# Attention and max-out FFN on one core: weighted sums two beats earlier in the first pairs, small bound products moved, GpSimd tied to the row maxima, first batch's maxima in SBUF

## The chip, the core and the metric

The kernel runs on one NeuronCore of a Trainium2 chip. The metric is the device time in microseconds (us). Before the change three runs took 1024.45, 1021.29 and 1019.76 us, with a median of 1021.29 us.

## The reference

Inputs are `q`, `k`, `v` of shape (8, 12, 448, 64), gains `g_q`, `g_k` of 64, and four 768 x 768 matrices. All are float32.

```python
q_n, k_n = rmsnorm(q, g_q), rmsnorm(k, g_k)       # over the last axis, eps 1e-6
scores = q_n @ k_n.T / 8
attn = exp(scores - rowmax); attn /= sum + 1e-9
x = (attn @ v), heads put side by side            # (8 * 448, 768)
h = max(x @ w1, x @ w2, x @ w3)
out = h @ w_out
```

## The kernel before

**Pairs and beats.** Two heads of one batch make a *pair*; there are 48, six to a batch. The program is one Python loop that writes the instructions of all five engines by hand, in order: each pair `g` has 12 *beats* `i`, and `beat(g, i)` (L1085) issues what is due there. `later(n, work)` puts a small step n beats on; those steps come at the end of their beat, in `tick`, and the ones marked `True` come last there. Each engine then takes its own instructions strictly in that order, so the order on each engine is the schedule, and the tile framework adds the semaphores between them.

**One pair.** The 448 query rows of a pair go in four chunks `c`, three beats each: three of 128 rows by two heads, and a last one in which 64 rows of each head share a tile (`banks(c)` is 1). For a chunk, `scores` (L655) lets TensorE write the score tile `sc` to PSUM (two buffers in all), `row_max` (L688) lets VectorE find the negated row maxima `nm`, and `softmax` (L697) lets ScalarE take the exponentials and row sums.

**The first six pairs** (`g < PLAIN`) run in float32, without the split in two terms. Their exponentials `e` are turned by TensorE (`turn_plain` L719, tiles `turned`), copied to `pt` by ScalarE (`keep_turned` L735), and multiplied with the values (`add_values` L832, tile `av`); q and k rows are turned likewise (`turn_whole` L522, tiles `rows`). The row sums are spread by small products (`spread_sums` L758), VectorE scales `av` (`scale_plain` L856), and `finish` (L861) writes the two float16 terms of the result, `xt`, on ScalarE and VectorE. All the small PSUM tiles (`turned`, `rows`, `spread`, `marks`, `most` and the FFN's `acc`) share one pool of three buffers, tag `m`, taken in turn. **The other 42 pairs** use float16 in two terms, and DMA does the turning; there a `sc` buffer is free only after VectorE's `lower_weights` (L802, instruction L806).

**Norms.** GpSimd squares the rows of pair g+2 (`squares`, L443), VectorE sums them (`sum_squares`, L450), GpSimd takes the inverse root (`inv_rms`: a scale at L460 and a power at L464) and scales the rows (`scale_rows`, L472).

**Weights.** While the first pairs run, 24 blocks of weights are decoded. A block comes in one DMA (`load_raw`), ScalarE rebiases it (L182), VectorE decodes it in three steps (L190, L194, L199). Every third block `bound_in` (L260) computes a bound: 18 small products into `marks` (L274), a row maximum (L162), a one-column product `most` (L283), a clear (L288) and a power on GpSimd (L293). Then ScalarE and VectorE split the three blocks in two float16 terms (L303, L306). `bound_block` and `bound_out` do the like for `w_out`, and `largest_v` with `bound_v` (L560, L589) for each batch of values: 12 products per half batch (L586), and a one-column product `most` (L597).

**FFN.** `thirds` (L993) feeds FFN steps to TensorE between the attention's steps; the first batch's FFN is queued at pair 6, beat 6, so until then TensorE has nothing but attention and bounds to do. `layer1` (L875) makes 18 units; for each, `hidden` (L887) takes the maximum of three products: the first is copied to SBUF (`m`, L890), the second is joined in `m`, the third is joined in the PSUM tile `acc` itself (L894), which L900 and L904 then read for the two terms of `ht`. So the third `acc` keeps its PSUM buffer until L904 has read it. `layer2` (L933) multiplies with `w_out` (L942).

## Time and profile before

| | |
|---|---|
| median of three runs | 1021.29 us (1019.76 to 1024.45) |
| the profiled execution: its own time, its span | 1023.19 us, 1021.3 us |
| TensorE busy (matmul) | 983.2 us, 96% |
| VectorE, ScalarE, GpSimd busy | 693.2, 624.1, 600.9 us |
| mean granted TensorE clock | 0.984 |
| TensorE busy in 0 to 240 us | 208.2 us |
| TensorE busy in 240 to 1021.3 us | 775.0 of 781.3 us |

The profile is one execution of the program. A row of the timeline has a start, a duration, the engine, the line of the program, `out<-in` and the shapes, and in brackets how long the engine had been idle before it and what released it. In the grouped view a row gives busy time and the mean of one instruction in ns, then the idle time just before the group. A windows row gives for a stretch of time the busy time of each engine, the granted TensorE clock (1.00 is full) and the DMA share. PE is TensorE, PEld its weight loads, DVE VectorE, ACT ScalarE, POOL GpSimd.

### The profile page before, as it was taken

How to read it: one execution, taken by the hardware profiler on the slowest of the kernel's cores; microseconds unless marked ns; L12 is line 12 of the kernel's file. 1: busy time of each engine (PE TensorE's matmuls, PEld its weight loads, DVE VectorE, ACT ScalarE, POOL GpSimd, SP SyncE). 2: the span in 40 equal slices, each digit the busy share in tenths (PEclk: the TensorE clock that was granted, in tenths of full speed). 3: DMA queues.
4: the chain of work that ended last, by engine and by line, in shares of the span. 5: the costliest groups of instructions: out<-in, count | busy, mean ns of one | idle time of the engine just before them, and what ended most of it. 6: DMA issues, size and time to landing. Idle time of an engine off the chain costs nothing. (4 is left out here: it accounts for less than half of the span.)

```text
span 1021.3 us, 17511 instructions
## 1 busy us (share of the span) xinstructions
PE 983.2 (96%) x6045; PEld 528.8 (52%) x6045; DVE 693.2 (68%) x1341; ACT 624.1 (61%) x1419; POOL 600.9 (59%) x659
## 2 busy tenths in 40 slices
PE   8987789899999999999999999999999999999998
PEld 5554444445555555555555555555555555555554
DVE  6998998788667767776677666776767757660120
ACT  6787776477566676666656675667666666651111
POOL 7666786567666576666676765776666657310000
PEclk9998799899999999999999999999999999999999
DMA  9955899979989899999989999999989998851001
GB/s 241 232 165 156 192 177 206 162 136 173 203 170 176 164 210 191 171 175 179 195 162 180 171 195 185 184 165 184 197 154 181 177 195 137 144 94 56 1 1 62
DMA packets 519548, 165.94 MB, mean 162 GB/s; under 512 B 494436, under 2 KB 515236, under 8 KB 519460
## 3 DMA queue, kind: packets, MB, share of 16 engines
q1 hardware_dynamic: 456480, 148.83, 75.3%
q10 hardware_dynamic: 62980, 16.00, 8.4%
q8 instruction: 48, 0.79, 0.3%
q14 instruction: 40, 0.33, 0.1%
HBM read 53.28 MB, written 11.01 MB: 63 GB/s over the span
## 5 line engine op out<-in xcount | busy, mean ns | idle before, releaser
L880 PE MATMUL acc<-xt,w_sb 128*128 128x448 f16 x2592 | 516.0, 354 | 3.6 <-DVE ht L904 3.3
L880 PEld LDWEIGHTS <-w_sb 128*128 128x128 f16 x2592 | 251.4, 98 | 246.4 <-issue 18.0
L709 ACT ACTIVATE sc<-sc,nm 128x448 f32<-128x448 f32 x294 | 178.8, 608 | 190.0 <-DVE nm L693 185.4
L693 DVE TENSOR_REDUCE nm<-sc 128x2 f32<-128x896 f32 x192 | 186.2, 970 | 102.2 <-PE sc L671 59.5
L796 ACT ACTIVATE pp<-sc,rs 128x448 f16<-128x448 f32 x294 | 173.0, 633 | 79.1 <-ACT sc L709 36.3
L806 DVE SCALAR_TENSOR_TENSOR pp<-sc,rs,pp 128x448 f16<-128x448 f32 x294 | 188.0, 675 | 1.7 <-ACT pp L796 1.6
L464 POOL TENSOR_TENSOR ri<-ri,half_neg 128x7 f32<-128x7 f32 x96 | 146.5, 1526 | 8.0
L942 PE MATMUL acc<-w_sb,ht 128*128 128x384 f16 x864 | 147.9, 326 | 0.0
L498 POOL TENSOR_TENSOR kp<-kn,kp 128x448 f16<-128x448 f32 x42 | 43.6, 1037 | 161.4 <-ACT kp L492 154.8
L671 PE MATMUL sc<-kt,qt 128*128 128x448 f16 x504 | 116.7, 354 | 4.0 <-DVE pp L806 3.2
L942 PEld LDWEIGHTS <-ht 128*128 128x128 f16 x864 | 83.7, 98 | 59.2 <-issue 3.9
L671 PEld LDWEIGHTS <-qt 128*128 128x128 f16 x504 | 49.0, 98 | 50.2 <-issue 4.9
L851 PE MATMUL av<-pt,vp 128*64 128x448 f16 x672 | 73.0, 355 | 1.7 <-DMA pt<-pp 1.7
L909 POOL COPY hx<-ht 128x128 f16<-128x128 f16 x48 | 15.4, 321 | 95.0 <-DVE ht L904 93.9
L866 DVE SCALAR_TENSOR_TENSOR xt<-av,xt 128x448 f16<-128x448 f32 x42 | 26.2, 625 | 59.8 <-ACT xt L865 59.8
L638 POOL TENSOR_TENSOR vp<-vr,vp 128x512 f16<-128x512 f32 x42 | 50.0, 1192 | 21.0 <-ACT vp L632 21.0
L450 DVE TENSOR_REDUCE ss<-sq 128x7 f32<-128x448 f32 x96 | 57.7, 601 | 6.4 <-ACT sq L441 4.3
L498 POOL TENSOR_TENSOR qp<-qn,qp 128x448 f16<-128x448 f32 x42 | 45.6, 1086 | 22.8 <-ACT qp L492 21.8
L851 PEld LDWEIGHTS <-vp 128*64 128x64 f16 x672 | 36.0, 109 | 35.8 <-issue 16.7
L460 POOL TENSOR_SCALAR ri<-ss 128x7 f32<-128x7 f32 x54 | 17.8, 329 | 60.4 <-DVE ss L450 59.7
L894 DVE TENSOR_TENSOR m<-acc,m 128x448 f32<-128x448 f32 x48 | 29.5, 615 | 33.2 <-PE acc L880 33.0
L900 ACT ACTIVATE ht<-acc 128x448 f16<-128x448 f32 x48 | 26.2, 546 | 41.8 <-DVE acc L894 41.8
(136 smaller groups left out, 1189.3 us busy)
## 6 DMA issues: line engine op xcount, KB each, us to landing
raw<-in_moe_w_dram SPq DMA_DIRECT2D x18, 768.0 KB, 5.2
kt<-kt SPq DMA_DIRECT2D x84, 112.0 KB, 2.5
out_dram<-osb SPq DMA_DIRECT2D x24, 384.0 KB, 2.7
vr<-in_v_dram SPq DMA_DIRECT2D x42, 192.0 KB, 4.2
kr<-in_k_dram ACTq DMA_DIRECT2D x34, 224.0 KB, 3.6
qr<-in_q_dram ACTq DMA_DIRECT2D x34, 224.0 KB, 4.4
raw<-in_moe_w_out_dram SPq DMA_DIRECT2D x6, 768.0 KB, 5.1
vs<-vp SPq DMA_DIRECT2D x84, 48.0 KB, 2.3
```

Source lines behind the costliest of these rows:

```text
L450: nc.vector.tensor_reduce(sums[g % 2][:, KQ[what]], sq, axis=AX, op=ALU.add)
L464: nc.gpsimd.tensor_tensor(out=ri, in0=ri, in1=half_neg[:, at], op=ALU.pow)
L498: nc.gpsimd.tensor_tensor(out=parts[:, :, 1], in0=n, in1=parts[:, :, 0], op=ALU.subtract)
L638: nc.gpsimd.tensor_tensor(out=vp[:, 1], in0=values_of(g).rearrange("p h n d -> p (h n) d"), in1=vp[:, 0], op=ALU.subtract,)
L671: nc.tensor.matmul(sc[:, h, :S], qt[:, 4 * h + c], kt[:, n, keys[h]], start=n == 0, stop=n == 1,)
L693: nc.vector.tensor_reduce(nm[:, :n], sc[:, :n, :S], axis=AX, op=ALU.max, negate=True)
L709: nc.scalar.activation(to, sc[:, h, :S], AF.Exp, bias=nm[:, h:h + 1], accum_out=total,)
L796: nc.scalar.activation(pp[:, h, 0], sc[:, h, :S], AF.Copy, scale=rs[:, h:h + 1])
L806: nc.vector.scalar_tensor_tensor(out=pp[:, h, 1], in0=sc[:, h, :S], scalar=rs[:, h:h + 1], in1=pp[:, h, 0], op0=ALU.mult, op1=ALU.subtract,)
L851: nc.tensor.matmul(av[half, :S], values, pt[:, 7 * h + block, SHIFT[h]:SHIFT[h] + S], start=n == 0, stop=n == len(steps) - 1,)
L880: nc.tensor.matmul(acc[:, :S], wt[:, wp, c], xs[c][:, xp], start=(c == 0 and n == 0), stop=(c == NCT - 1 and n == 2),)
L942: nc.tensor.matmul(acc[:, :HW], lhs, wo_sb[:, f, wp, half * HW:(half + 1) * HW], start=(f == 0 and n == 0), stop=(f == NFT - 1 and n == 2),)
```

## The change

It has four parts.

1. **Weighted sums two beats sooner.** In the first pairs `add_values` comes at beat 2 of the next pair and not at beat 4. For that the last chunk is turned at beat 11 of its own pair (it was beat 0 of the next), and `keep_turned` of it comes at beat 0, ahead of the next pair's first exponentials on ScalarE.
2. **Small products moved.** `bound_in`'s one-column product and its clear come two beats later, and with them the splits L303 and L306; `bound_block` and `bound_out` come one to three beats later; `largest_v` of the first batch comes two or three beats later. `bound_v` of the later batches starts six beats sooner (beat 7 of the pair ahead), and its product comes four beats after its maximum instead of two.
3. **GpSimd follows the row maxima.** In the first six pairs, ahead of each `row_max`, VectorE clears one element (`here`) and GpSimd copies it, so that what stands behind that copy on GpSimd starts when VectorE starts the row maximum. The squares, inverse roots and scaled rows are re-dealt to the beats with a row maximum, one large GpSimd step behind each copy.
4. **First batch's maxima in SBUF.** For batch 0 the third join writes to `m` in SBUF instead of `acc`, and L900 and L904 (L909 and L913 after) read `m`.

```diff
+    def follow():
+        here = sb.tile([1, 1], F32, name="here", bufs=4)
+        nc.vector.memset(here, 0.0)
+        nc.gpsimd.tensor_copy(seen, here)
...
-            later(8, bound_out, True)
+            later(10, bound_out, True)
...
-        later(6, products)
-        later(8, lambda: row_largest(o_row[:, ft:ft + 1], box[0][:, 0:P]), True)
+        later(7, products)
+        later(9, lambda: row_largest(o_row[:, ft:ft + 1], box[0][:, 0:P]))
...
-        for at, work in ((2, products), (4, reduce), (5, spread), (7, clear)):
+        for at, work in ((2, products), (4, reduce), (7, spread), (9, clear)):
...
-        for at, work in ((2, across), (3, spread), (5, scale)):
+        for at, work in ((2, across), (4, spread), (6, scale)):
...
-        later(2, spread)
-        if b < SQUARED:
-            later(3, clear)
-        later(5 if b < SQUARED else 3, scale)
+        if b >= SQUARED:
+            later(4, spread)
+            later(5, scale)
+            return
+        for at, work in zip((4, 6, 9) if b else (2, 3, 5), (spread, clear, scale)):
+            later(at, work)
...
-        most = m if j == 1 else acc[:, :S]
+        most = m if j == 1 or b == 0 else acc[:, :S]
...
+        if i == 0 and 0 < g <= PLAIN:
+            keep_turned(w, 3)
...
-            if 0 < k <= 4 * PLAIN:
-                turn_plain(*divmod(k - 1, 4))
+            if g < PLAIN:
+                if c > 0:
+                    turn_plain(g, c - 1)
...
+                if g < PLAIN:
+                    follow()
                 row_max(*divmod(k + 1, 4))
...
-        if w >= 0 and i == (4 if w < PLAIN else 7):
+        if w >= 0 and i == (2 if w < PLAIN else 7):
             add_values(w)
...
+        if g < PLAIN:
+            if i in (2, 5):
+                squares(n, "kq"[i // 3])
+            if i == 11:
+                turn_plain(g, 3)
+            if i in (4, 7):
+                sum_squares(n, "kq"[i // 7])
+            if i in (5, 8):
+                if i == 8:
+                    scale_rows(n, "k")
+                inv_rms(n, "kq"[i // 8])
+            if i == (9 if n >= PLAIN else 11):
+                scale_rows(n, "q")
+        elif n < G:
...
-            later(8, lambda: largest_v(i // 3))
+            later(10 if i == 0 else 11, lambda: largest_v(i // 3))
...
-        if g == 1 and i == 1:
+        if g == 1 and i == 4:
             bound_v(0)
-        if g > 1 and g % NP == 0 and g < G and i == 1:
-            bound_v(g // NP)
+        if g % NP == NP - 1 and g + 1 < G and i == 7:
+            bound_v(g // NP + 1)
```

**What moves on the engines.** TensorE, where pair 3 ends and pair 4 begins (`sc` are scores, `turned` the turned exponentials, `rows` the turned k, `most` the bound's product, `av` the weighted sum). Before:

```order
L663 MATMUL sc<-kt,qt 128x448 x2
L729 MATMUL turned<-ident,e 112x128 x8
L663 MATMUL sc<-kt,qt 128x448 x2
L729 MATMUL turned<-ident,e 112x128 x4
L527 MATMUL rows<-ident,kn 128x128 x3
L532 MATMUL rows<-ident,kn 64x64 x2
L663 MATMUL sc<-kt,qt 128x448 x2
L729 MATMUL turned<-ident,e 112x128 x8
L840 MATMUL av<-pt,vr 64x448 x8
```

After, at the same place:

```order
L672 MATMUL sc<-kt,qt 128x448 x2
L738 MATMUL turned<-ident,e 112x128 x8
L290 MATMUL most<-most,ones_c 128x1
L738 MATMUL turned<-ident,e 112x128 x4
L672 MATMUL sc<-kt,qt 128x448 x2
L534 MATMUL rows<-ident,kn 128x128 x3
L539 MATMUL rows<-ident,kn 64x64 x2
L849 MATMUL av<-pt,vr 64x448 x8
L672 MATMUL sc<-kt,qt 128x448 x2
```

The weighted sum now stands ahead of the third score tile, which needs the new pair's first exponentials; the last four turns stand ahead of the second score tile; and `most`, which stood ahead of the first of these rows, has moved between the turns.

GpSimd, one pair's worth in the middle of the first six pairs. Before:

```order
L460 TENSOR_SCALAR ri<-ss_129 128x7
L464 TENSOR_TENSOR ri<-ri,half_neg 128x7
L472 TENSOR_TENSOR kn<-kr,ri 128x448
L472 TENSOR_TENSOR qn<-qr,ri 128x448
L293 TENSOR_TENSOR w_up<-most,half_neg 128x1
L294 TENSOR_SCALAR w_up<-w_up 128x1
L443 TENSOR_TENSOR sq<-kr 128x448
L443 TENSOR_TENSOR sq<-qr 128x448
```

After:

```order
L450 TENSOR_TENSOR sq<-kr 128x448
L165 COPY seen<-here 1x1
L450 TENSOR_TENSOR sq<-qr 128x448
L467 TENSOR_SCALAR ri<-ss_130 128x7
L471 TENSOR_TENSOR ri<-ri,half_neg 128x7
L165 COPY seen<-here 1x1
L479 TENSOR_TENSOR kn<-kr,ri 128x448
L467 TENSOR_SCALAR ri<-ss_130 128x7
L471 TENSOR_TENSOR ri<-ri,half_neg 128x7
L165 COPY seen<-here 1x1
L479 TENSOR_TENSOR qn<-qr,ri 128x448
```

The large steps stood in twos; now each has a copy of its own ahead of it, and that copy waits for VectorE.

More of the change, by code (lines that the diff above doesn't have):

```diff
@@ L158, in qknorm_attention_maxout_ffn_kernel @@
     sums = [const.tile([P, 2 * UNITS], F32, name=f"ss{i}") for i in range(2)]
+    seen = const.tile([1, 1], F32, name="seen")
+    def follow():
+        here = sb.tile([1, 1], F32, name="here", bufs=4)
+        nc.vector.memset(here, 0.0)
+        nc.gpsimd.tensor_copy(seen, here)
     def row_largest(dst, src):
@@ L1096, in beat @@
                 scores(*divmod(k + 1, 4))
-            if 0 < k <= 4 * PLAIN:
-                turn_plain(*divmod(k - 1, 4))
+            if g < PLAIN:
+                if c > 0:
+                    turn_plain(g, c - 1)
+            elif k == 4 * PLAIN:
+                pass
             elif 0 < k <= 4 * G:
@@ L1101, in beat @@
         if part == 1:
-            if 0 < k <= 4 * PLAIN:
-                keep_turned(*divmod(k - 1, 4))
+            if c > 0 and g < PLAIN:
+                keep_turned(g, c - 1)
             if PLAIN <= g < G:
@@ L1125, in beat @@
         thirds(of[i] + (len(queue) > 1 and i % 6 == 4))
-        if w >= 0 and i == (9 if w < PLAIN else 10):
+        if w >= 0 and i == (9 if 0 < w < PLAIN else 10):
             finish(w, x_of[w // NP])
@@ L1148, in beat @@
             upper_rows(n, "k")
-        if n < G:
+        if g < PLAIN:
[12 more added lines that the diff above has]
+        elif n < G:
             if i in (0, 3):
```

## The prediction

> **What bounds the kernel now.** I read the busy time of four stretches, then TensorE's waits up to 320 us, then the timeline at the longest of them, then the groups of VectorE's instructions.
>
> ```profile
> 25.20:118.60 93.40, 81.10 (x580) 46.30 (x580) 86.41 (x120) 73.45 (x164) 63.40 (x56) 0.91 0.70 181
> 118.60:134.00 15.40, 10.28 (x64) 6.60 (x64) 14.62 (x28) 10.38 (x25) 9.76 (x9) 0.78 0.84 201
> 134.00:240.00 106.00, 96.21 (x581) 49.22 (x581) 91.00 (x172) 70.49 (x151) 73.72 (x76) 0.97 0.93 173
> 240.00:1021.30 781.30, 774.98 (x4676) 412.89 (x4672) 485.52 (x990) 454.12 (x1047) 434.70 (x496) 1.00 0.84 156
> PE sc L663 <- ACT e L709: 11.4, 6, 2.9
> PE most L597 <- DVE v_most L591: 4.9, 1, 4.9
> PE marks L586 <- DMA vr<-in_v_dram: 1.6, 2, 1.2
> PE marks L586 <- DVE o_up L342: 1.3, 1, 1.3
> PE most L337 <- DVE o_most L333: 0.8, 1, 0.8
> ```
>
> The four windows rows give span, then busy PE, PEld, DVE, ACT, POOL, then clock. From 240 us on TensorE stands still for only 781.3 - 775.0 = 6.3 us, so nothing the change does there can bring much. Pairs 1 to 5 lie in 25.2 to 118.6: there VectorE is the fullest (86.4 of 93.4 us), TensorE has 81.1, and the clock is at 0.91. The whole kernel ends when TensorE has done its fixed work, so every us that TensorE loses early, standing or at a low clock, is lost at the end.
>
> The timeline shows what one such wait is:
>
> ```profile
> 46.56 3.23 PE L840 MATMUL av<-pt,vr 112*64 112x448 f32 x16
> 76.02 1.02 PE L663 MATMUL sc<-kt,qt 64*128 64x448 f32 x4
> 81.22 1.87 PE L663 MATMUL sc<-kt,qt 64*128 64x448 f32 x4 [2.54 <-ACT e L709]
> 98.33 1.08 ACT L742 COPY pt<-turned 112x512 f32<-112x512 f32 x2
> 99.22 1.08 DVE L693 TENSOR_REDUCE nm<-sc 128x2 f32<-128x896 f32 x1
> 101.73 1.87 PE L663 MATMUL sc<-kt,qt 64*128 64x448 f32 x4 [2.94 <-ACT e L709]
> 105.41 4.44 PE L840 MATMUL av<-pt,vr 112*64 112x448 f32 x16
> ```
>
> At the end of pair 4 TensorE has turned the last chunk and wants the third score tile of pair 5, whose buffer is free when the first exponentials are done; these wait for the row maximum, which stands in VectorE's full queue until 99.22. TensorE stands 2.94 us; then its clock is halved, the scores take 1.87 us for 1.02 and the weighted sum 4.44 for 3.23. The weighted sum, ready long before, stood behind the wait.
>
> **The change part by part.**
>
> *The weighted sum ahead (pairs 2 to 5).* 3.2 us of products now lie where TensorE stood 2.5 to 2.9 us. They need the last chunk's turns (now ahead of the second scores) and its copies on ScalarE, which now come ahead of the new exponentials. New waits: the last turns take the PSUM buffer of the first half of the chunk before, so they wait for the first of the two copies of 98.33 (by my estimate from that row and ScalarE's order some 1 to 2 us of standing, less than the 2.54 us that halved the clock), and the exponentials wait for those turns and their copies. What is late next is VectorE, so I count the stage on VectorE:
>
> ```profile
> 31.59 0.55 DVE L190 TENSOR_SCALAR w_sb<-raw 128x768 uint32<-128x768 uint32 x1
> 34.58 0.95 DVE L199 SCALAR_TENSOR_TENSOR w_sb<-raw,w_sb 128x768 uint32<-128x768 uint32 x1
> 47.68 1.01 DVE L306 SCALAR_TENSOR_TENSOR w_sb<-w_sb,w_up 128x768 f16<-128x768 f32 x1
> L199 DVE SCALAR_TENSOR_TENSOR w_sb<-raw,w_sb 128x768 uint32<-128x768 uint32 x16 | 18.0, 1126 | 0.1
> L693 DVE TENSOR_REDUCE nm<-sc 128x2 f32<-128x896 f32 x16 | 17.3, 1081 | 0.0
> L194 DVE SCALAR_TENSOR_TENSOR w_sb<-raw,w_sb 128x768 uint32<-128x768 uint32 x15 | 17.2, 1148 | 0.3
> L306 DVE SCALAR_TENSOR_TENSOR w_sb<-w_sb,w_up 128x768 f16<-128x768 f32 x12 | 12.8, 1062 | 0.0
> L190 DVE TENSOR_SCALAR w_sb<-raw 128x768 uint32<-128x768 uint32 x15 | 11.4, 758 | 0.0
> 91.27 0.29 DVE L162 TENSOR_REDUCE most<-marks 128x1 f32<-128x128 f32 x1 [2.64 <-PE marks L274]
> 93.13 0.29 DVE L162 TENSOR_REDUCE v_rows<-marks 128x1 f32<-128x128 f32 x1 [1.57 <-PE marks L586]
> ```
>
> VectorE's idle time of 7.0 us in the stretch (93.4 - 86.4) is mostly these two waits, 2.64 + 1.57 = 4.2 us, for products that ran late in pair 4 after the half clock of 81.22. With that hole gone I take 4.2 us off.
>
> *GpSimd follows.* The four grouped rows of the weights' decode and split are longer in the mean than undisturbed ones: 16 x (1126 - 950) + 15 x (1148 - 950) + 12 x (1062 - 1010) + 15 x (758 - 550) ns = 2.8 + 3.0 + 0.6 + 3.1 = 9.5 us. The row maximum, which reads PSUM, is 1.08 us always, so GpSimd's large steps do it no harm; each now starts with one. I take 70% of the 9.5 away, 6.6 us (the bounds are 0 and 9.5): a large step is 0.94 us alone and starts a hand-over and a small copy after the maximum, so its end overlaps the next step by some 0.2 us, about 3 x 0.2 x 5 pairs = 3 us.
>
> ```profile
> 0.92 0.06 DVE L140 MEMSET ones_c<- 128x1 f32 x1
> 33.92 1.49 POOL L464 TENSOR_TENSOR ri<-ri,half_neg 128x7 f32<-128x7 f32 x1
> 91.13 0.94 POOL L472 TENSOR_TENSOR qn<-qr,ri 128x448 f32<-128x448 f32 x1
> 174.94 0.29 POOL L909 COPY hx<-ht 128x128 f16<-128x128 f16 x1 [0.23 <-DVE rs L789]
> ```
>
> The added clears: 21 of the 24 lie in the stretch, at 0.06 us 1.3 us (up to 4 at 0.2). The copies (nearest row 0.29) are GpSimd's, which has 30 us free here. The risk is behind them: everything on GpSimd now waits for VectorE's queue, and VectorE's sums of squares wait for GpSimd. I put 1.0 us for new waits of that kind.
>
> The power at 33.92 ran through while the L199 of 34.58 stayed at 0.95 us, so powers cost VectorE nothing here. The Trainium skill, page "SBUF — State Buffer", section "Who interferes with whom", holds otherwise: a VectorE step with two SBUF inputs and a GpSimd step that reads SBUF exclude each other for the whole of whichever began first; by that the powers behind the copies would each stop a decode step. The trace speaks against it for the powers, and for the 0.94 us steps it agrees. That rule is a rival below.
>
> *Bounds later.* One L306 fewer is done ahead of pair 6, -1.0 us there and +1.0 after. Stretch sum: -4.2 - 6.6 + 1.3 + 1.0 - 1.0 = -9.5 us: 83.9 us for five pairs. TensorE fits: its 81.1 us hold half-clock spells such as 1.87 for 1.02 and 4.44 for 3.23, at least 2.1 us each. In the first 25 us the late values' 1.6 us no longer stand in front; VectorE is nearly full there, so 0.5 of it.
>
> *Pair 6 until the FFN.*
>
> ```profile
> 122.80 6.11 PE L840 MATMUL av<-pt,vr 112*64 112x448 f32 x16
> 131.97 1.26 DVE L806 SCALAR_TENSOR_TENSOR pp<-sc,rs,pp 128x448 f16<-128x448 f32 x2
> 134.04 0.57 PE L678 MATMUL sc<-kt,qt 128*64 128x448 f16 x4
> ```
>
> The 4.9 us wait is the largest, but its removal brings nothing: the FFN starts behind the scores of 134.04, which need L806 at 131.97, and VectorE, busy 14.6 of the 15.4 us from 118.6, has the same work and one L306 more: +1.0. TensorE will have done its sum early and stand about 4 us here instead; the half clock then falls on the FFN's first products. The spell after 122.3 cost 6.11 - 3.23 = 2.9 us; VectorE is still nearly full then (91.0 of 106.0 us from 134), so that TensorE's loss is in part hidden, and I put +1.0 here: +2.0 in all (-2 to +4).
>
> *Maxima in SBUF, and the output bound.*
>
> ```profile
> 184.82 2.43 PE L880 MATMUL acc<-xt,w_sb 128*128 128x448 f16 x12
> 186.69 0.62 DVE L894 TENSOR_TENSOR acc<-acc,m 128x448 f32<-128x448 f32 x1
> 188.22 1.26 DVE L806 SCALAR_TENSOR_TENSOR pp<-sc,rs,pp 128x448 f16<-128x448 f32 x2
> 190.20 0.62 DVE L904 SCALAR_TENSOR_TENSOR ht<-acc,ht 128x448 f16<-128x448 f32 x1
> 190.88 2.40 PE L880 MATMUL acc<-xt,w_sb 128*128 128x448 f16 x6 [3.29 <-DVE ht L904]
> 193.08 1.70 PE L671 MATMUL sc<-kt,qt 128*128 128x448 f16 x4
> 194.57 3.46 PE L880 MATMUL acc<-xt,w_sb 128*128 128x448 f16 x12
> ```
>
> With `m` in SBUF the buffer is free at 187.3 and not at 190.8. Of 3.3 us about 0.7 stays (the six products, 1.2 us, end at 188.8, and the scores behind them wait for L806 until 189.5): -2.6. The half clock behind it goes: 2.40 for six products instead of 1.2, 3.46 for twelve instead of 2.43, and half of the scores' 1.70 between: 1.2 + 1.0 + 0.8, -3.0. The output bound's two waits (0.8 + 1.3) have their steps later or behind other products: -2.1, of which I give back 0.6, since `w_out`'s splits come three beats later and the first batch's second layer may meet them: -1.5. A second copy of `m` is held longer; it has two buffers and is refilled three units on, so nobody waits.
>
> *Sum.* -0.5 - 9.5 + 2.0 - 5.6 - 1.5 = -15.1 us; after 240 us, 0. The profiled execution took 1023.2 us with a span of 1021.3; 1023.2 - 15.1 = 1008.1. Its own time is 1.9 us above the median of the runs, so for the median I say **1006 us**. Half a per cent is 5.1 us, about what a measurement of this kernel can tell from no change.
>
> **The rivals.**
>
> *Contention stays (0.15).* GpSimd comes late to its starts: between the second and third copy of a pair it has 0.94 + 0.2 + 1.5 us and more, where VectorE has about 3 us (1.08 + 0.95 + 0.29 + 0.55 and the sum itself); a start late by one us meets the decode again. Then the 6.6 us stay and 1.3 are added: 1006 + 7 = 1013. For: GpSimd waits for VectorE's decode steps too. Against: the large step stands first behind each copy. *Powers stop the decode (0.04).* If the powers behind the copies did hold VectorE, two in each of five pairs at some 1 us of their 1.49, it is 10 us: 1016; the row of 34.58 is against it. This is the Trainium skill's rule above.
>
> *The hole moves (0.18).* If the last turns wait longer than reckoned for the copies (ScalarE has the result's copy, a rebias and these copies in front), TensorE stands over 2.5 us there, and the clock halves in pairs 2 to 5 as before: at 2.1 us and more in three of them, about 6 us: 1012. The Trainium skill, page "TensorE: Matmul & The Clock Gate", section "HAM oscillation — how this bites in real kernels", puts the harmful gap above about 3.4 us; by that alone the spells behind the holes of 2.5 to 2.9 us would have another cause and stay, and the sum would be some 6 us less. The trace's 2.54 us wait halved the clock already, so its row decides.
>
> *Slower (0.04).* GpSimd becomes the link that VectorE waits for: each sum of squares stands in VectorE's queue ahead of the next row maximum, 1.6 us behind a copy's release at the nearest (maximum 1.08, small step, decode 0.55), while copy and square take 0.29 + 0.94 and two hand-overs. There are 12 sums in six pairs. From a delay of 15/12 = 1.3 us each the gain is gone; at a whole power and a copy, 1.49 + 0.29 = 1.8 us each, it is 21 us: 1027.
>
> *It does nothing to the holes (0.05):* the moved products wait for the same exponentials through ScalarE's order: only the SBUF and output terms, -7: 1014.
>
> **How the numbers follow.** Forecast 0.54: 1000 to 1011 (contention terms between 0 left and half left, pair 6 between -2 and +4 around 1006). The four cases of 1012 to 1016 hold 0.42, slower 0.04. The range 999 to 1016 leaves out the slower case and the upper tails, about 0.15. Faster by over 0.5% is below 1016.2: 0.85; within 0.5% 0.10; slower 0.05.
>
> **What would show it.** Right: no TensorE wait over 2 us between 25 and 115 us, clock 1.00 there; the four decode rows' means within 0.1 us of 0.95, 0.95, 1.01 and 0.55; pairs 1 to 5 in 84 us; a TensorE wait of 3 to 5 us ahead of the FFN; none on `acc` near 180 us. Wrong: sums of squares (L457) waiting for GpSimd; the half clock in pairs 2 to 5; pairs 1 to 5 above 89 us; TensorE idle after 240 us above 8 us.

## The result, and the profile after

The changed kernel takes 1017.35 us in the median of 8 runs (1015.57 to 1019.06), beside it the kernel before 1022.68 us (1019.76 to 1026.11): a ratio of 0.9948, 95% interval 0.9929 to 0.9967. So it is faster by 5.3 us; 15.1 us were forecast. The profiled execution took 1017.4 us, with a span of 1015.6 us.

The busy time of four stretches, cut at the same events as before (row maximum of pair 6, last scores of pair 6, then 240 us); the columns are those of the first view of the prediction:

```profile
25.10:111.20 86.10, 74.94 (x581) 44.45 (x579) 82.82 (x140) 72.92 (x163) 60.78 (x75) 0.98 0.74 196
111.20:127.40 16.20, 9.90 (x58) 5.68 (x56) 15.38 (x29) 9.62 (x23) 14.30 (x15) 0.72 0.82 196
127.40:240.00 112.60, 102.87 (x624) 53.24 (x625) 96.52 (x184) 75.46 (x163) 78.89 (x78) 0.97 0.90 170
240.00:1015.60 775.60, 769.13 (x4637) 410.24 (x4635) 481.57 (x979) 451.05 (x1040) 431.06 (x492) 1.00 0.84 156
```

Pairs 1 to 5 became 7.3 us shorter (93.4 to 86.1), pair 6 took 0.8 us more. The third stretch, which began 6.6 us sooner, hardly gained: TensorE stood for 9.7 of its 112.6 us, as it stood for 9.8 of 106.0 before, at a clock of 0.97 both times. TensorE's waits up to 320 us:

```profile
PE sc L680 <- DVE pp L815: 9.8, 7, 3.0
PE turned L738 <- ACT pt L751: 8.0, 6, 2.1
PE sc L687 <- DVE pp L815: 3.3, 1, 3.3
PE sc L672 <- ACT e L718: 2.6, 2, 1.6
PE marks L593 <- DVE o_row L169: 2.6, 1, 2.6
```

The 11.4 us for the exponentials and the 4.9 us for the bound of the values are gone or small. In their place TensorE waits for VectorE's lower halves of the attention weights (9.8 + 3.3 us, where it was 3.0 before), six times for ScalarE's copies of the turned exponentials (8.0 us), and once for `o_row`, which is new. The timeline around that one:

```profile
127.41 0.96 PE L687 MATMUL sc<-kt,qt 128*64 128x448 f16 x4 [3.27 <-DVE pp L815]
128.30 2.42 PE L889 MATMUL acc<-xt,w_sb 128*128 128x448 f16 x6
144.88 1.30 PE L889 MATMUL acc<-xt,w_sb 128*128 128x448 f16 x6
148.42 0.28 DVE L169 TENSOR_REDUCE o_row<-marks 128x1 f32<-128x128 f32 x1
148.75 1.41 PE L593 MATMUL marks<-vr 128*128 128x128 bf16 x12 [2.56 <-DVE o_row L169]
149.96 2.44 PE L889 MATMUL acc<-xt,w_sb 128*128 128x448 f16 x6
```

The row bound of an output block is read a beat later than before, behind a row maximum and two lower halves; until then it holds one of the three PSUM buffers. TensorE stands 2.56 us, and the six first-layer products behind it take 2.44 us where those of 144.88 took 1.30. The same happens behind the 3.27 us wait of pair 6.

To see where the lead comes and goes, I take the start of the last chunk's scores of each pair. The executions on record reach the first of them at 17.6 to 18.8 us; so all are counted from that of pair 0. The *lead* is how much sooner than in the kernel before an event comes.

| us from the last scores of pair 0 to those of pair | 5 | 6 | 7 | 8 | 9 | 10 | 12 |
|---|---|---|---|---|---|---|---|
| before | 93.95 | 116.10 | 136.79 | 157.43 | 182.12 | 203.28 | 239.62 |
| changed | 84.42 | 109.43 | 136.46 | 154.36 | 175.45 | 196.09 | 234.87 |
| lead | 9.5 | 6.7 | 0.3 | 3.1 | 6.7 | 7.2 | 4.8 |

The gain up to pair 5 is there. By the end of pair 7 all of it is given back. What is left at the end comes from pairs 8 and 9, where the wait on `acc` at 190.9 is gone, less 2.4 us in pairs 11 and 12. That is the question of the experiments.

### The profile page after: what moved, and what is told of

It is laid out like the page before. It is cut to its first block, busy times and chain, and to the rows that moved or that the text cites. A ratio compares the mean times of both kernels' runs of the same rounds, so it can differ in the third digit from the quotient of the medians.

```text
span 1015.6 us, 17562 instructions
## 1 busy us (share of the span) xinstructions
PE 977.4 (96%) x6045; PEld 527.5 (52%) x6045; DVE 692.9 (68%) x1365; ACT 624.7 (62%) x1419; POOL 602.4 (59%) x683
## 3 DMA queue, kind: packets, MB, share of 16 engines
q1 hardware_dynamic: 456480, 148.83, 75.5%
## 4 chain that ended last, share of the span: by engine, by line
PE 60%; DMA 1%; DVE 0%; ACT 0%; issue 0%; SPq 0%
PE acc L889 34%; PE acc L951 12%; PE av L860 6%; PE sc L680 6%; PE sc L687 1%; DMA pt<-pp 0%; DVE pp L815 0%; DMA out_dram<-osb 0%; ACT osb L960 0%; DVE nm L702 0%; ACT pp L805 0%; ACT qp L499 0%; PE most L604 0%; ACT ht L909 0%; SPq L834 0%
## 5 line engine op out<-in xcount | busy, mean ns | idle before, releaser
L702 DVE TENSOR_REDUCE nm<-sc 128x2 f32<-128x896 f32 x192 | 186.2, 970 | 99.4 <-PE sc L680 58.5
L903 DVE TENSOR_TENSOR m<-acc,m 128x448 f32<-128x448 f32 x54 | 33.1, 614 | 33.1 <-PE acc L889 33.0
L488 POOL TENSOR_TENSOR qn<-qn,gain 128x448 f32<-128x448 f32 x42 | 49.0, 1167 | 3.3
L467 POOL TENSOR_SCALAR ri<-ss 128x7 f32<-128x7 f32 x54 | 20.1, 373 | 51.1 <-DVE ss L457 49.9
```

The costliest lines, as they stand in the source:

```text
L702: nc.vector.tensor_reduce(nm[:, :n], sc[:, :n, :S], axis=AX, op=ALU.max, negate=True)
```

## The experiments

The theories: A, the new waits of TensorE (A1: the half clock behind them) cost the lead; B, VectorE's work sets the pace, whatever wait is removed; C, VectorE's steps run longer beside GpSimd, so GpSimd's load counts; D, only the sooner sums and the maxima hold a gain.

All were timed against the kernel before on the same chip, in 5 rounds. The ratio is to the kernel before; the lead is over its profiled execution, at the same events as above. A lead belongs to one execution: the profiled one of e13 took 3.2 us more than that run's median and that of e6 1.9 more, those of e7 and e18 1.7 and 2.4 less.

| run | median us | ratio, 95% | lead at pair 5 | 7 | 9 | 12 |
|---|---|---|---|---|---|---|
| the change | 1017.35 | 0.9948 (0.9929 to 0.9967) | 9.5 | 0.3 | 6.7 | 4.8 |
| e5 values alone | 1018.52 | 0.9969 (0.9955 to 0.9983) | 7.0 | 3.2 | 5.0 | 5.0 |
| e13 copies, GpSimd alone | 1023.73 | 1.0018 (1.0003 to 1.0034) | -0.8 | -3.4 | -3.9 | -3.9 |
| e17 small products alone | 1021.91 | 1.0004 (0.9990 to 1.0017) | 2.2 | -3.1 | 0.4 | -0.5 |
| e14 SBUF alone | 1019.95 | 0.9989 (0.9977 to 1.0002) | -0.5 | -1.0 | 4.4 | 2.1 |
| e15 values and SBUF | 1016.84 | 0.9964 (0.9951 to 0.9978) | 6.8 | 4.1 | 9.4 | 7.1 |
| e18 the same, shared bound | 1017.38 | 0.9953 (0.9934 to 0.9971) | 6.4 | 3.3 | 8.7 | 6.9 |
| e2 change without copies | 1018.66 | 0.9970 (0.9956 to 0.9983) | 7.9 | -0.4 | 6.1 | 4.2 |
| e3 change, maxima in PSUM | 1019.04 | 0.9970 (0.9955 to 0.9985) | 9.9 | 0.7 | 3.9 | 3.0 |
| e1 change, output bounds back | 1017.22 | 0.9954 (0.9937 to 0.9971) | 9.8 | 3.2 | 6.7 | 3.4 |
| e10 change, row bounds back | 1017.25 | 0.9962 (0.9947 to 0.9976) | 8.9 | 3.5 | 7.5 | 4.5 |
| e4 change, 40 + 40 products | 1016.57 | 0.9960 (0.9947 to 0.9973) | 9.5 | 1.2 | 6.3 | 5.1 |
| e11 change, 95 + 130 products | 1016.05 | 0.9949 (0.9933 to 0.9964) | 8.9 | 0.7 | 7.8 | 5.8 |
| e16 e15 and 95 + 130 products | 1019.70 | 0.9983 (0.9972 to 0.9994) | 5.9 | -0.5 | 5.2 | 2.9 |
| e6 change, no sums of q | 1020.23 | 0.9986 (0.9973 to 1.0000) | 8.5 | -3.0 | 3.2 | 0.3 |
| e7 change, no squares | 1016.00 | 0.9953 (0.9935 to 0.9971) | 11.3 | 4.4 | 10.9 | 8.9 |
| e8 change, splits on GpSimd | 1018.55 | 0.9969 (0.9958 to 0.9980) | 8.3 | -0.2 | 5.5 | 3.6 |
| e9 change, one power | 1017.87 | 0.9969 (0.9959 to 0.9980) | 9.5 | -1.9 | 4.6 | 2.7 |
| e12 e9, e10 and e11 | 1020.05 | 0.9990 (0.9979 to 1.0000) | 9.7 | 3.3 | 7.1 | 4.2 |

### The wait at 148.75: e1, e10, e17

```diff
-        later(7, products)
-        later(9, lambda: row_largest(o_row[:, ft:ft + 1], box[0][:, 0:P]))
+        later(6, products)
+        later(8, lambda: row_largest(o_row[:, ft:ft + 1], box[0][:, 0:P]), True)
```

e1 also has the shared bound at its old beats; e17 is the kernel before with all moved small products (and the first pair's `finish` a beat later, as in the change) and nothing else.

> The changed kernel with the row bounds of the output blocks and the shared output bound put back to the beats they had before (products 6, reading 8 and last in its beat, shared bound 8 with steps 2, 3, 5); all else is as changed. Theory A (pair 7 gave its lead back because the later o_row reading holds a buffer in PSUM, and TensorE stood 2.57 us ahead of the value products at 148.75 and then ran at half clock): that wait goes, the start of the last scores of pair 7 comes 3 to 4 us earlier than 154.4, and the kernel takes about 1013.5 us (ratio to the changed kernel 0.996 to 0.997). Rival B (VectorE's queue bounds pairs 6 and 7, and whatever wait is taken away, another takes its place): the checkpoint moves by under 1 us and the kernel stays at 1017 us.

> The changed kernel with the row bounds of the output blocks alone put back (products 6, reading 8 and last in its beat); the shared output bound stays as changed. In the run with both put back, the last scores of pair 7 came 3.24 us earlier, of which 0.3 were left at pair 8, and then 2.0 us were lost in pair 10 to two waits on the shared bound. If those two were the price of the shared bound's old beats, the last scores of pair 10 stand at 214 or earlier here and the kernel takes 1015.5 to 1017; if they come from the row bounds, pair 10 ends near 216 again and the kernel takes 1017 to 1018. Whatever the wait at 148.75 cost, the lead of pair 7 is gone at pair 8 again if VectorE's load sets the pace there.

> The kernel before with only the small products and bounds of the values and of the weights at their later beats (with the first pair's finishing a beat later, as it waits for the values' bound). If VectorE's 4.2 us of waiting in pair 4 was a matter of these products, the last scores of pair 5 come 3 us or more before 111.9 and the kernel takes about 1018. If they hold nothing (theory D), it takes 1020 to 1023.

Pairs 6, 7 and 8 of e10 by busy time (span, PE, PEld, DVE, ACT, POOL, clock), then pair 7 of e17, and from e17's waits of TensorE the one on `o_row`:

```profile
103.82:128.84 25.02, 15.43 (x102) 9.48 (x100) 24.16 (x43) 16.93 (x38) 21.86 (x23) 0.82 0.75 190
128.84:152.06 23.22, 21.40 (x124) 10.76 (x126) 21.73 (x39) 17.39 (x37) 17.68 (x18) 0.90 0.92 187
152.06:172.91 20.85, 18.83 (x118) 9.39 (x115) 18.76 (x32) 12.57 (x28) 13.61 (x13) 1.00 0.84 178
```

```profile
131.65:157.69 26.04, 22.53 (x130) 11.76 (x132) 23.19 (x42) 18.10 (x38) 20.29 (x20) 0.87 0.92 192
```

```profile
PE marks L586 <- DVE o_row L162: 2.6, 1, 2.6
```

Half of theory A holds. The small products make pair 7 long: e17's takes 26.0 us where the kernel before takes 20.7, with the same wait, and with the row bounds alone put back pair 7 of the changed kernel takes 23.2 us and not 27.0. But the end does not come sooner. Pair 8 then takes 20.9 us where it took 17.9, and by pair 9 e1 has the lead of the changed kernel and e10 0.8 us more. Theory A, that the wait cost the lead for good, falls. Of e1, the loss in pair 10 (23.0 us) is the shared bound's: e10 has 21.6.

What is lost for good shows when all runs are set side by side. Pairs 7 and 8 together take 42.3 to 45.8 us in the thirteen kernels with the small products moved (in e1 and e10 all but the output or the row bounds), and 39.9 to 42.1 us in the seven that have not (before, e5, e13 to e16, and e18, which moves the shared bound only). VectorE is busy 39.5 to 40.9 us there in the first group and 37.7 to 38.7 in the second. The two pairs of e10, then of e5, at nearly the same clock:

```profile
128.84:172.91 44.07, 40.23 (x240) 20.16 (x241) 40.49 (x71) 29.96 (x64) 31.29 (x30) 0.95 0.89 183
131.00:172.96 41.96, 39.81 (x240) 20.11 (x240) 37.86 (x72) 28.67 (x62) 31.12 (x33) 0.94 1.01 196
```

VectorE makes five splits in these pairs of the change, e10 and e17, and four before, in e5 and in e15. Pairs 11 and 12 tell the same: 38.8 us with all small products moved, 36.3 to 36.8 without, 37.7 in e18 and 37.8 in e1. So part 2 of the change costs some 3 us in pairs 7 and 8 (2.6 in e17) and 2.4 in pairs 11 and 12, of which 1.0 is the shared bound's. In e1 the output bounds are back and pairs 7 and 8 still take 44.1 us; so the products of `bound_in` or of the values' bounds cost there, and which of them is open.

### The half clock: e4, e11, e16

```diff
+                if g == PLAIN and i in (5, 8):
+                    fill(st[w]["av"], 95 if i == 5 else 130)
                 scores(*divmod(k + 1, 4))
```

`fill` issues products of 64 columns into columns of the weighted sums' bank that nobody reads; e4 has 40 of them at each place.

> The changed kernel with 40 matrix products without a reader ahead of the scores of chunks 2 and 3 of pair 6 (the two places where TensorE stands 3.04 and 3.27 us), written to unused columns of the bank of the weighted sums; they add work and remove no wait. Theory A1 (the half clock behind these waits is what costs, 2.42 us against 1.30 for six first-layer products at 128.30): the granted clock is 1.00 there, the feed-forward products of pair 7 start at full clock, and the kernel takes 2 to 3 us less, about 1014.5. Rival B (VectorE's queue decides, TensorE catches up anyway): the clock is up, the last scores of pair 7 start where they did (154.4 within 1 us), and the kernel stays at 1017 us; if the products outlast the holes, a little above.

> The changed kernel with 95 and 130 matrix products without a reader (about 3.2 and 4.3 us at full clock) ahead of the scores of chunks 2 and 3 of pair 6, so that TensorE is busy through both waits; with 40 each, 1.9 and 3.1 us of waiting were left and six first-layer products at 127.8 still took 2.42 us. Theory A1 (the half clock behind the waits costs 2 to 3 us for good): six products take 1.30 us there, the last scores of pair 7 come 2 us or more before 154.4, and 1 us or more of that is left at pair 12. Rival: what TensorE gains at full clock, it waits for VectorE later; at pair 9 the lead is under 0.5 us.

> The same with 95 and 130 products without a reader in the two waits of TensorE in pair 6. If the half clock behind those waits costs, it takes 1 to 2 us less than the run without them; if VectorE takes it back, it is level with it within 0.5 us.

Five microseconds at the start of the feed-forward in e11 by busy time and clock, then from e11's timeline the first six products and the next wait; last, the same five microseconds in the changed kernel:

```profile
125.00:130.00 5.00, 4.55 (x122) 3.73 (x119) 4.80 (x10) 2.41 (x6) 4.13 (x4) 1.00 0.72 152
```

```profile
129.26 1.31 PE L893 MATMUL acc<-xt,w_sb 128*128 128x448 f16 x6
134.22 0.73 PE L893 MATMUL acc<-xt,w_sb 128*128 128x448 f16 x3 [1.46 <-DVE o_row L173]
```

```profile
125.00:130.00 5.00, 2.59 (x9) 0.92 (x10) 4.60 (x9) 3.68 (x8) 4.84 (x6) 0.50 0.60 110
```

The clock went from 0.50 to 1.00 and six products from 2.42 to 1.31 us, as meant. Then TensorE met a new wait of 1.46 us on VectorE, and the lead at pair 7 grew by 0.4 us, at pair 12 by 1.0. So the half clock behind these waits is worth about 1 us, as the prediction had it, not 2 to 3; the runs (0.9949 and 0.9948) cannot tell it from nothing. With 40 products (e4) the six products still took 2.42 us. In e16 and e12 the 130 products came behind another wait of 2.1 and 2.2 us and took 5.5 us, in part at half clock, and 4.0 us at full clock, which TensorE did not have: pair 6 became 30.0 and 28.4 us long, and the kernels slower.

### VectorE's load and GpSimd beside it: e2, e6, e7, e8, e9, e12, e13

```diff
# e2
-                if g < PLAIN:
-                    follow()
# e6
-            if i in (4, 7):
-                sum_squares(n, "kq"[i // 7])
+            if i == 4:
+                sum_squares(n, "k")
...
# e7, squares()
+        if 2 <= g < PLAIN + 2:
+            return
# e7, sum_squares()
+        if 2 <= g < PLAIN + 2:
+            row_largest(sums[g % 2][:, KQ[what]], st[g][what + "r"])
+            return
# e8, lower()
+                if n % NJ == 0:
+                    nc.gpsimd.tensor_scalar(
+                        out=f, in0=f, scalar1=up, scalar2=1.0, op0=ALU.mult, op1=ALU.mult
+                    )
+                    nc.gpsimd.tensor_tensor(
+                        out=w_sb[:, n, 1], in0=f, in1=w_sb[:, n, 0], op=ALU.subtract
+                    )
+                    return
# e9, inv_rms()
...
+            if what == "q":
+                ri = s["ri"]
+                nc.gpsimd.tensor_tensor(out=ri, in0=ri, in1=half_neg, op=ALU.pow)
...
```

e6 and e7 leave work out and serve for their times alone. e13 puts `follow()` and the re-dealt beats of GpSimd's steps, and nothing else, into the kernel before. e12 is e9 with the edits of e10 and e11.

> The changed kernel without the GpSimd copies behind the row maxima (and the small memsets that feed them); the small products, the weighted sums and the maxima in SBUF stay as changed. If the prediction's contention term holds (6.6 us of longer VectorE decode steps taken away, at 1.3 us for the memsets), the row maximum of pair 6 comes about 5 us later than 111.2, and the kernel takes about 1022 us, less what pairs 6 and 7 then no longer give back. Rival: the copies move GpSimd's work no better than its own queue did, the decode steps keep their means, and the row maximum of pair 6 stands within 1.5 us of 111.2 (1016 to 1018 us in all).

> The kernel before with GpSimd's work re-dealt over the beats and the copies behind the row maxima, and nothing else. By the prediction's contention term (6.6 us less of decode time, 1.3 us more of memsets) the last scores of pair 6 come about 5 us before 134.0 and the kernel takes about 1016 to 1018. By the runs so far (means of L194 down by 0.18 us, of L199 and L306 up by 0.05 and 0.03) the sum over the decode groups falls by about 2 us and the memsets take 1.4 of it back: 1020 to 1022, within 0.2% of before.

> The changed kernel without the sums of squares of the queries of pairs 2 to 7 (six VectorE reductions of 0.61 us, 3.6 us of VectorE work taken out of pairs 0 to 5; GpSimd's powers then no longer wait for them). Theory B (VectorE's work, not a wait, sets the pace from pair 1 to pair 8, so a moved step comes back and only a step that is gone is gained): the last scores of pair 6 come 3 to 4 us earlier than 127.4, those of pair 9 at least 2.5 us earlier than 193.4, and the kernel takes about 1014. Theory A (the new waits and the half clock behind them cost the lead): pairs 6 and 7 lose what they lost before, the lead is gone at pair 9, and the kernel stays at 1017.

> The changed kernel without GpSimd's squares of pairs 2 to 7 (twelve GpSimd products of 0.9 to 1.6 us); VectorE reduces the rows themselves by largest magnitude, in the same number of reductions of the same size. So only GpSimd's share beside VectorE falls. If what is left of the decode steps' excess (means of 1.18, 0.96 and 0.72 us against shortest ones of about 0.95, 0.95 and 0.55) is contention with GpSimd, the means fall by a third or more of the excess, up to 3 us over pairs 1 to 6, and the end comes 2 to 3 us earlier. Rival (the excess comes from the DMA transfers and ScalarE's reads, or from other GpSimd work): the means stay within 0.03 us and the kernel at 1017 us.

> The changed kernel with the lower half of every third first-layer weight block made by GpSimd in two steps instead of by VectorE in one (six VectorE steps of 1.0 to 1.1 us taken away, about 6 us by pair 8; GpSimd gets twelve steps of some 1.7 us, an estimate from its 128x448 products of 0.94 to 1.04 us). Theory B (VectorE's work sets the pace): if GpSimd's idle time of about 5.5 us a pair takes it, the last scores of pair 9 come 4 us or more earlier than 193.4 and the kernel takes about 1013 us, less than both. Rival: GpSimd's own chain (squares, powers, rows) comes late, VectorE waits for it or runs longer beside it, and the kernel takes 1017 us or more.

> The changed kernel with one GpSimd power over the 14 columns of keys and queries of a pair in place of two over 7, for pairs 2 to 7 (and one scaling step ahead of it in place of two, for pairs 2 to 5). Powers of 7 columns took 1.74 us and of one column 1.04 us here, so one of 14 takes about 2.55 us, an estimate; a pair then needs 3.4 us instead of 5.1, about 10 us less GpSimd work over six pairs. Theory C (VectorE's decode steps run longer beside GpSimd, whatever GpSimd does there; without the squares 12.8 us less of GpSimd gave 4.1 us less of VectorE up to pair 6): VectorE is busy about 3 us less up to pair 6, the last scores of pair 6 come about 3 us before 127.4 and the kernel takes about 1014. Rival: the powers keep VectorE off by their number of elements and not by their time, so that nothing is gained (1017), or the later keys make TensorE wait (above 1018).

> The three edits together: one power for keys and queries, the row bounds put back, and products without a reader in both waits of pair 6. If theory C holds and the edits add up, it takes 1012 to 1014 us, less than both kernels; if VectorE's load from pair 6 to pair 10 takes back what a single wait gives, 1015 to 1017.

The stretch from the last scores of pair 0 to those of pair 6, in the kernel before, the changed one, e13, e5 and e6 (the first number is the span, the one after PEld VectorE's busy time):

```profile
17.94:134.04 116.10, 96.56 (x686) 55.96 (x684) 108.30 (x157) 90.62 (x202) 79.96 (x70) 0.90 0.75 187
```

```profile
17.98:127.41 109.43, 89.84 (x679) 53.36 (x677) 105.30 (x178) 89.34 (x199) 80.72 (x95) 0.94 0.78 198
```

```profile
18.45:137.36 118.91, 97.59 (x686) 56.72 (x684) 104.64 (x178) 90.68 (x202) 81.11 (x94) 0.88 0.71 181
```

```profile
18.49:131.00 112.51, 91.91 (x688) 56.79 (x686) 110.11 (x155) 90.67 (x202) 83.51 (x69) 0.93 0.74 191
```

```profile
18.46:131.24 112.78, 89.64 (x679) 53.91 (x677) 104.38 (x171) 89.51 (x199) 85.02 (x95) 0.93 0.77 190
```

VectorE's busy and idle time: 108.3 + 7.8 before, 104.6 + 14.3 with the copies alone, 110.1 + 2.4 with the sums alone, 105.3 + 4.1 with all. The copies and the re-dealt steps do shorten the decode: the four groups of the prediction take 71.5 us in this stretch before and 67.5 in e13, with one step of 0.7 fewer, so 3.2 us less, of which the clears take 1.4. But alone they gain nothing, since TensorE's holes stay and VectorE stands 6.5 us more, waiting for TensorE and ScalarE. The sums take those waits away, and the four groups then take 73.8 us (one step fewer too), 3.0 more. Alone, each part loses to the other some of what it gains. Together they do better: at pair 6 the leads of e5, e13 and e17 are 3.6, -2.8 and 2.3 us, and that of the change is 6.7.

e2 tests the copies with all else in place. Up to pair 6 the four groups take 69.0 us without them and 67.8 with them: 1.2 us gained, where the clears take 1.4 and VectorE's busy time is the same (105.4 and 105.3 us). The row maximum of pair 6 comes 1.8 us later (counted from pair 0), neither the 5 us of the term nor the 1.5 or less of its rival. The lead without them is 1.6 us smaller at pair 5 and 0.6 at pair 12, and the intervals of the two ratios overlap.

e6 shows the same trade. 3.6 us of VectorE's work were gone, but it was busy only 0.9 us less than in the changed kernel (L201 rose from 962 to 1151 ns in the mean, L313 from 1089 to 1142) and idle 4.3 us more, most of it here (0.7 us in the changed kernel):

```profile
DVE ss L457 <- POOL sq L450: 3.2, 2, 1.9
```

So theory B, as forecast, falls too: this work taken from VectorE alone brought nothing. Nor did work given to GpSimd (e8: its subtraction took 2.15 us, and the splits left on VectorE 1.31). Theory C stands on e7 alone. The decode groups of e7 up to pair 6:

```profile
L206 DVE SCALAR_TENSOR_TENSOR w_sb<-raw,w_sb 128x768 uint32<-128x768 uint32 x19 | 20.3, 1068 | 0.3
L201 DVE SCALAR_TENSOR_TENSOR w_sb<-raw,w_sb 128x768 uint32<-128x768 uint32 x19 | 19.0, 998 | 0.1
```

With 12.8 us of GpSimd's products gone the lead is 10.9 us at pair 9 and 8.9 at pair 12, 4.1 more than the change has. But the profiled execution is the shortest of its six (1014.3 to 1019.4 us), and the medians and intervals do not part the two kernels. e9 shows the trade again: up to pair 6 VectorE was busy 101.3 us, 4.0 less than in the changed kernel as theory C has it, but idle 5.4 us more. One power of 14 columns took 2.74 us, and the later keys made TensorE wait 1.6 us at 27.8. The three edits of e12 did not add up either: 1020.1 us, where 1012 to 1014 were forecast.

### The maxima and the pieces that pay: e3, e5, e14, e15, e18

```diff
# e14; e3 is the reverse on the changed kernel
-        most = m if j == 1 else acc[:, :S]
+        most = m if j == 1 or b == 0 else acc[:, :S]
# e5
-        if w >= 0 and i == (4 if w < PLAIN else 7):
+        if w >= 0 and i == (2 if w < PLAIN else 7):
             add_values(w)
# e18, beside e15
-            later(8, bound_out, True)
+            later(10, bound_out, True)
-        for at, work in ((2, across), (3, spread), (5, scale)):
+        for at, work in ((2, across), (4, spread), (6, scale)):
```

e5 also has the turns and copies of a pair's last chunk where the change puts them; e15 is e5 and e14 together.

> The changed kernel with the first batch's maxima written to PSUM again, as before the change. If the prediction's term for them holds (5.6 us), TensorE waits again on a VectorE or ScalarE reader ahead of a first-layer product near 180 us and the kernel takes about 1023 us, level with the kernel before. Rival: with the other edits the wait near 180 us does not come back, and the kernel stays within 2 us of 1017.

> The kernel before with only the weighted sums of the plain pairs two beats sooner (with the last chunk's transposes and copies that they need); GpSimd's work, the small products and the maxima are as before. The prediction's idle term (4.2 us of VectorE waiting in pair 4) was given to the small products and the sums together; if the sums carry it, the start of the last scores of pair 5 comes about 4 us earlier than 111.9 and the kernel takes about 1018 us. Rival (the sums don't matter, the moved small products and maxima do): pair 5 stays within 1.5 us of 111.9 and the kernel within 2 us of the one before.

> The kernel before with the first batch's maxima kept in SBUF, and nothing else. By the prediction's term (2.6 us of wait near 190 and 3.0 us of half clock behind it) the kernel takes about 1016. By the run that undid it on the changed kernel (1.8 to 2 us) it takes about 1019.5.

> The kernel before with the weighted sums two beats sooner and the maxima in SBUF: the change without its copies, without the re-dealt GpSimd work and without the moved small products. If those three hold nothing (theory D), it takes 1015.5 to 1017.5, level with the whole change or less. If the copies hold the 1.5 us that undoing them cost, it takes 1018 to 1019.

> The kernel before with the weighted sums two beats sooner, the maxima in SBUF and the shared output bound at its later beats (10, then 4 and 6). Without the last, it took 1016.8 and its pair 10 took 23.0 us, with waits of 1.7 and 1.3 us on the bound. If those waits go as in the changed kernel, pair 10 takes 20.6 to 21.6 us and the kernel 1014.5 to 1015.5, less than both. If pair 11 or 12 takes it back, it stays at 1016.5 to 1017.

Pairs 9 and 10 of e14 by busy time, two of TensorE's waits in its pair 10, then pair 10 of e18:

```profile
175.90:195.70 19.80, 18.16 (x112) 9.14 (x112) 17.25 (x34) 13.94 (x33) 14.57 (x17) 1.00 1.01 185
195.70:218.72 23.02, 19.42 (x126) 9.93 (x124) 19.71 (x40) 14.23 (x31) 17.34 (x18) 1.00 1.01 174
```

```profile
PE most L337 <- DVE o_most L333: 1.7, 1, 1.7
PE marks L586 <- DVE o_up L342: 1.3, 1, 1.3
```

```profile
191.04:212.68 21.64, 19.38 (x126) 9.91 (x122) 17.06 (x35) 12.48 (x29) 16.68 (x18) 1.00 0.94 175
```

The maxima make pair 9 4.9 us shorter (24.7 to 19.8), near the 5.6 forecast; pair 10 is 1.9 us longer (21.2 to 23.0), with two waits on the shared output bound. With the maxima in PSUM again in the changed kernel (e3), the wait on `ht` is back: pair 9 takes 24.2 us for 21.1, of which pair 10 gives 1.1 back. The shared bound's later beats bring pair 10 to 21.6 us (e18), and pair 12 takes 18.6 us for 17.8. e15 agrees with theory D: the sooner sums and the maxima have a larger lead than the whole change at pair 9 (9.4 and 6.7 us) and at pair 12 (7.1 and 4.8), without copies, re-dealing or moved products. Its profiled execution then waited 2.0 us for a transposing transfer in pair 13, and from there on its lead is like that of the change, 5 to 6 us. e13 and e17, the parts that it leaves out, gain nothing alone (1.0018 and 1.0004). The intervals of e15 and the change overlap, so a tenth or two of a per cent may still be held by those parts. No run is faster than the changed kernel by more than its interval, so no better version is claimed.

## Why the prediction was wrong

Two steps failed. The contention term was to bring 6.6 us and brought 2.5, and without the copies (e2) some 1.2 us of it are lost. And the moved small products, entered as a gain, cost some 3 us in pairs 7 and 8 and 2.4 in pairs 11 and 12. The maxima in SBUF and the output bound brought 3 us less than their terms.

The terms of the sum against the profiled executions, by the events above (us; minus is sooner):

| stretch | forecast | measured |
|---|---|---|
| up to pair 1 | -0.5 | -0.1 |
| pairs 1 to 5 | -9.5 | -7.3 |
| pair 6 until the FFN, and the half clock behind it | +2.0 | +0.8 until the FFN |
| pairs 7 and 8 | no other term | +3.6 |
| pairs 9 and 10 (maxima, output bound) | -7.1 | -4.1 |
| pairs 11 and 12 | 0 | +2.4 |
| from there to the end | 0 | -1.0 |
| all | -15.1 | -5.7 |

**Direction and bound: right.** The gain is won before 240 us, and TensorE's idle time after it is 6.5 us (6.3 before).

**The sum ahead: right.** The holes before the third scores are gone, the turns wait 1.0 to 1.7 us as reckoned, and VectorE's idle time in the stretch fell by 3.7 us (7.0 to 3.3), where 4.2 less 1.0 for new waits were forecast. "No wait over 2 us" holds but for one of 2.08 us. The clock was not 1.00 but 0.98: it halved once, behind a wait of 1.70 us.

**Contention, -6.6 us: the first step that failed.** The groups of pairs 1 to 5:

```profile
L206 DVE SCALAR_TENSOR_TENSOR w_sb<-raw,w_sb 128x768 uint32<-128x768 uint32 x16 | 18.7, 1167 | 0.3
L201 DVE SCALAR_TENSOR_TENSOR w_sb<-raw,w_sb 128x768 uint32<-128x768 uint32 x15 | 14.5, 968 | 0.1
L313 DVE SCALAR_TENSOR_TENSOR w_sb<-w_sb,w_up 128x768 f16<-128x768 f32 x11 | 12.1, 1104 | 0.0
L197 DVE TENSOR_SCALAR w_sb<-raw 128x768 uint32<-128x768 uint32 x15 | 10.5, 701 | 0.0
L164 DVE MEMSET here<- 1x1 f32 x20 | 1.2, 59 | 0.0
```

The excess is 16 x 217 + 15 x 18 + 11 x 94 + 15 x 151 ns = 7.0 us, after 9.5: 2.5 us gained and 1.2 paid for the clears. One group of four was freed. The rows show two of the reasons:

```profile
106.38 0.61 DVE L702 TENSOR_REDUCE nm<-sc 128x1 f32<-128x448 f32 x1
107.11 0.93 POOL L479 TENSOR_TENSOR kn<-kr,ri 128x448 f32<-128x448 f32 x1
107.45 1.41 DVE L313 SCALAR_TENSOR_TENSOR w_sb<-w_sb,w_up 128x768 f16<-128x768 f32 x1
109.01 2.07 POOL L471 TENSOR_TENSOR ri<-ri,half_neg 128x7 f32<-128x7 f32 x1
109.76 0.96 DVE L206 SCALAR_TENSOR_TENSOR w_sb<-raw,w_sb 128x768 uint32<-128x768 uint32 x1
```

```profile
41.76 2.31 POOL L471 TENSOR_TENSOR ri<-ri,half_neg 128x7 f32<-128x7 f32 x1
42.65 1.09 DVE L702 TENSOR_REDUCE nm<-sc 128x2 f32<-128x896 f32 x1
44.17 0.93 POOL L479 TENSOR_TENSOR qn<-qr,ri 128x448 f32<-128x448 f32 x1
44.31 1.21 DVE L197 TENSOR_SCALAR w_sb<-raw 128x768 uint32<-128x768 uint32 x1
```

The row maximum of a last chunk takes 0.61 us and not 1.08, "always"; GpSimd's product, which starts 0.7 us behind it, is over at 108.04, and the split beside it takes 1.41 us. I had reckoned with the long maxima only. These short ones account for 1.4 us of the excess, in five rows. More of it, 2.5 us in four rows, comes from products that start late: at 42.65 GpSimd is still in a power, its product starts 1.5 us behind the maximum, when that is over, and a decode step of 0.55 takes 1.21 us. Another 1.7 us, in two rows, lie beside products in pair 5 that have no copy of their own. Where a product starts 0.4 us behind a long maximum, the next step loses 0.15 us, near the 0.2 reckoned. The remark on powers held: the decode step beside the power of 109.01 takes 0.96 us, and it is the power that grows, from 1.49 to 2.07 us. So the rival "contention stays" came true by more than half, late starts included, and that of powers did not; the rule of the Trainium skill on which it stood (page "SBUF — State Buffer", section "Who interferes with whom": the first of the two blocks the other) is nearer to GpSimd's products here, 0.4 us longer for 0.6 us of overlap, than to its powers.

**Idle time and contention added up.** I summed -4.2 and -6.6 as if they were independent; e13 and e5 show that they are not. This is not what made the sum too large: in the whole change both terms were gained, 3.7 and 2.5 us, and the second was small by itself.

**The moved small products, counted as a gain: the step that cost most.** The sum gives them -0.5 and -1.5, and one late split +1.0. The lead fell from 7.4 us at the row maximum of pair 6 to 0.3 at pair 7: +7.1 us, of which 2.8 came back in pair 8. Pair 6 itself behaved (+0.8, with waits of 3.0 and 3.3 us where 3 to 5 were foreseen). What I missed starts in pair 7: I moved the row bounds by a beat at no cost and did not ask which PSUM buffer they hold meanwhile. In e17 pair 7 is 5.4 us longer than before; e10 shows that putting them back does not help by itself. VectorE is busy 92% of pairs 6 to 8 after and 94% before (64.4 of 69.9 us, 60.0 of 63.5), and the change brings 4.4 us more into these pairs: a row maximum, a split, a decode step and a sum of squares that the kernel before had done earlier. So part of the lead at pair 5 was work put off.

In e5 and e15, which put off nearly as much (63.3 and 63.2 us busy in these pairs), it is paid in pair 6, where their lead falls by 3.4 and 3.0 us; pairs 7 and 8 then cost e5 0.6 us and gain e15 0.8. The rest of the loss goes with the small products: 3.6 us in pairs 7 and 8 and 2.4 in pairs 11 and 12, for which the sum had nothing. By themselves (e17) they lead by 2.2 us at pair 5, -0.3 at pair 8, 1.9 at pair 10 and -0.5 at pair 12, and end level. That it is VectorE's added work in pairs 7 and 8 that TensorE waits for is argued from the busy times; no run moves that work alone.

**Maxima in SBUF, -5.6 us: right in place, too large at the end.** Pair 9 gained 3.6 us in the change and 4.9 alone, but the whole kernel only 0.1% alone, which its interval does not part from nothing, and 0.2% on top of the rest (e3), as pair 10 and its output bound were next in line. **Output bound, -1.5 us:** e18 has -1.4 in pair 10 and +0.9 in pairs 11 and 12.

## What to carry to other kernels

A small step moved by a beat is priced by the buffer that it holds and by the stage into which its followers fall, not by its duration: here the moved products gained early and lost as much later. A lead is real only where the work behind it is done; before counting a faster stage, compare what the fullest engine has executed at the same event. And two savings on one engine, less waiting and less contention, act on each other: run each alone, and run the whole without each, before giving either a price.

## What the runs showed of the hardware

- TensorE's clock halved behind waits of 1.7 us, and not each time. Five microseconds behind a wait of 1.70 us at 58.5 us in the changed kernel, then the same place in e10, behind a wait of 1.75 us, and the next, behind 1.96 us at 75.5:

```profile
60.00:65.00 5.00, 5.00 (x23) 2.10 (x23) 4.97 (x8) 3.80 (x10) 3.02 (x6) 0.66 1.00 248
```

```profile
60.00:65.00 5.00, 5.00 (x31) 1.86 (x27) 4.97 (x10) 4.26 (x11) 2.79 (x6) 1.00 0.91 242
74.00:79.00 5.00, 3.51 (x11) 1.70 (x11) 4.97 (x9) 4.85 (x13) 4.45 (x6) 0.66 1.24 236
```

  The granted clock is 0.66, 1.00 and 0.66. From the last scores of pair 2 to those of pair 3 it took 17.7 us in the one and 16.6 us in the other. The Trainium skill, page "TensorE: Matmul & The Clock Gate", section "HAM oscillation — how this bites in real kernels", puts the harmful gap above 3.4 us; here the clock halved behind single waits of 1.7 to 2.6 us. It may be why one kernel's runs scatter over 3 us; that was not tried.
- A power on GpSimd with 7 columns took 1.49 us undisturbed and up to 2.3 us beside VectorE's decode steps, and with 14 columns 2.74 us in the mean. It did not lengthen VectorE's steps. GpSimd's 128x448 products did: from 18 to 127 us every decode or split step, before and after, that took over 0.06 us more than the shortest of its kind overlapped one. In the changed kernel a step lost 0.15 us where they overlapped by 0.3, and 0.86 where by 1.0.
